# Negating and splitting the softmax maxima: ScalarE and GpSimd in place of VectorE

## The chip, the core and the metric

The kernel runs on one core of a Trainium2 chip, in one launch. The core has a matrix engine (TensorE, PE in the profile, with its weight loads as PEld), VectorE (DVE), ScalarE (ACT), GpSimd (POOL) and SyncE (SP), which here issues every transfer. Each engine runs its own queue in order and waits for the others by semaphores. The metric is the device time of one execution in microseconds (us), the median of several runs.

## The reference

One transformer block with adaptive layer norm on x of 2048 x 512 in float32, with 32 heads of 16 and a hidden width of 1792. Cut to what matters:

```python
h = layernorm(x) * (1 + ca) + sa                    # sa, ca, ga, ... from silu(c) @ w_mod
q, k, v = split(h @ wqkv)                           # 32 heads x 2048 x 16
p = softmax(einsum("bhqd,bhkd->bhqk", q, k) * 16 ** -0.5)
x = x + ga * (einsum("bhqk,bhkd->bhqd", p, v) @ wo)
h = layernorm(x) * (1 + cb) + sb
u = h @ w1 + b1
x = x + gb * ((u * tanh(softplus(u))) @ w2)
```

The softmax subtracts the largest score of each query before the exponential. That maximum is what the change is about.

## The kernel before

The scores are computed twice. A first pass (`max_tile`, product L471, reduction L473) computes tiles of 128 queries x 512 keys and takes each row's maximum on VectorE. A second pass (`score`, product L512) computes them transposed, 128 keys x 512 queries, and ScalarE takes the exponential straight out of PSUM (L520). The maximum has to be subtracted per query, which is a column there; so it goes in as two extra rows of the product's inner dimension: `qa` holds the minus maximum in rows 48 and 49 of each half, and `ka` holds ones. Products run in a format of reduced precision (float32r), so the number is split: row 48 takes the rounded minus maximum, row 49 what the rounding left.

Work is cut into 32 repeats, n = 0 to 31: a block of 512 queries (4 of them) times a group of four heads (8 of them). A repeat has 16 steps t, and step t has two half-steps 2t and 2t+1. In one step TensorE issues four score products of this repeat, four products of the maxima for a later repeat (the maxima run 20 steps ahead, `PRO`), a share of a unit of the projections or of the MLP (L132), and eight products with the values (L540, called by `pv`), which end the step. The score and maximum tiles take turns in a ring of six PSUM banks (`ring`); a product waits until the engine that reads the bank's last tile has done so. The program's order is the order in which the Python code records instructions; `at(h, f)` records f when the recording reaches half-step h. Nothing reorders it later.

Once a repeat, `neg_max` reduces the maxima to 128 x 32 (L482) and hangs `max_rows` on the end of step 16n-4, behind its L540 products and so just ahead of the next step's products. `max_rows` takes two ring banks, transposes the maxima on TensorE (L490), and turns them into `mt`, 32 rows of 128 numbers: sixteen rows of rounded minus maxima (`lows` is 0) and sixteen of remainders (`lows` is -1). `put` stands at half-step 32n-5 and sends `mt` with four transfers of 4 KB (L501) to rows 48 and 49 of the two `qa` tiles of repeat n, in the order (head pair 0, half 0), (0, 1), (1, 0), (1, 1). The scores of the repeat begin at step 16n, with half 1 of pair 0 and then half 1 of pair 1, so the second score product reads what the fourth transfer brings.

GpSimd meanwhile works through the MLP's activation: for each unit a clamp (L740), a product (L754, L755), a quotient (L770 to L774) and a split (L95, L98), each stage hung on its own half-step, with ScalarE's exponentials and logarithms (L746, L758, L761) between them. It also adds results to the residual (L893, which reads `yd`; ScalarE writes `yd` at L892, and there is one such buffer).

Of the kernel before, what the change touches and what calls it, by code (L numbers as in the profile page):

```python
# [8 lines left out]
F32 = mybir.dt.float32  # L9
F32R = mybir.dt.float32r  # L10
AF = mybir.ActivationFunctionType
ALU = mybir.AluOpType
# [6 lines left out]
def adaln_block(ctx: ExitStack, tc: tile.TileContext, x, wqkv, wo, w1, b1, w2, c, w_mod, out):  # L19
    nc = tc.nc  # L20
# [56 lines left out]
    lows = cst.tile([P, 1], F32, name="lows")  # L77
# [69 lines left out]
    def ring(w=1):  # L147
        if w == 2 and ring_at[0] % 2:
            ring_at[0] += 1
        b = ring_at[0] % NRING  # L150
        ring_at[0] += w
        return ring_t[:, b, :] if w == 1 else ring_t[:, b:b + 2, :]
# [32 lines left out]
    def at(h, f):  # L185

        hooks.setdefault(h, []).append(f)
# [289 lines left out]
    def neg_max(n):  # L477

        mx = mxs.pop(n)
        mm = ap.tile([P, 4, 2, 4], F32, tag="mm", name="mm", bufs=2)  # L480
        twice = bass.AP(tensor=mx.tensor, offset=mx.offset, ap=[list(mx.ap)[0], [16, 4], [0, 2], [4, 4], [1, 4]])
        nc.vector.tensor_reduce(out=mm, in_=twice, op=ALU.max, axis=AX.X)  # L482
        ats.setdefault(16 * n + 16 - PRO, []).append(lambda: max_rows(n, mm))

    def max_rows(n, mm):
        t = ring(2)
        cols = mm.rearrange("p a v q -> p (a v q)")
        for g in range(2):
            r = slice(64 * g, 64 * g + 64)
            nc.tensor.transpose(t[:32, g, :64], cols[r], ident[r, r])  # L490
        pt = t[:32, :, :64]
        mh, mt = [ap.tile([32, P], F32R, tag=n_, name=n_, bufs=1) for n_ in ("mh", "mt")]
        halves = [m.rearrange("p (g q) -> p g q", g=2) for m in (mh, mt)]
        nc.vector.tensor_scalar_mul(halves[0], pt, -1.0)
        nc.vector.scalar_tensor_tensor(halves[1], halves[0].bitcast(F32), lows[:32], pt, op0=ALU.mult, op1=ALU.subtract)

        def put():
            for j in range(2):
                for s in range(2):
                    o = (2 * s + j) * 8  # L500
                    nc.sync.dma_start(  # L501
                        qa[(2 * n + j) % NR][64 * s + 48:64 * s + 50, :].rearrange("v (s q) -> v s q", s=4).bitcast(F32),
                        mt[o:o + 8, :].bitcast(F32))
        at(2 * (16 * n + 16 - PRO) + 3, put)
# [835 lines left out]
    t = T + 2  # L1340
# [32 lines left out]
```

## Time and profile before

| what | value |
|---|---|
| median of 3 runs | 1700.25 us (1697.17 to 1701.53) |
| the profiled execution | 1693.26 us, its span 1691.5 us |
| granted TensorE clock | 0.996 |
| busy: TensorE, VectorE, ScalarE, GpSimd | 98%, 85%, 78%, 53% |
| a usual step of the long middle part | 2.84 us |
| L494 and L495 on VectorE | 32 times 279 ns and 335 ns |

A row of the timeline gives the start and the length in us, the engine, the line, what is written and read, and in brackets the idle time of that engine ahead of it with what ended it. A row of groups gives, after the bar, the busy time in us, the mean length in ns, and the idle time ahead. Line numbers are those of the kernel before; L494 and L495 are also, in the changed kernel, the two operations that take their place.

### The profile page before, as it was taken

Reading aid. Unit: us, or ns where it says so; the run is one execution under the profiler, and the core shown is the slowest. Engines: PE = TensorE matmul, PEld = TensorE weight load, DVE = VectorE, ACT = ScalarE, POOL = GpSimd, SP = SyncE. Lnnn points to the kernel's source line nnn. Section 1 sums busy time; section 2 is a strip of 40 time slices with the busy share of each in tenths; the row PEclk is TensorE's granted clock in tenths of the full one; section 3 lists DMA queues with packets and bytes.
Section 4 is the critical chain, followed back from the end, with each engine's and each line's share of the span. In section 5 each row is a group of like instructions: output and inputs, shape, how many; then the busy total and the mean of one; then the engine's idle time right before and its main releaser. Section 6 shows DMA issues by size and latency. Waiting matters only on the chain.

```text
span 1691.5 us, 32962 instructions
## 1 busy us (share of the span) xinstructions
PE 1660.6 (98%) x12316; PEld 921.7 (54%) x12316; DVE 1429.9 (85%) x2362; ACT 1327.1 (78%) x2559; POOL 898.0 (53%) x906
## 2 busy tenths in 40 slices
PE   6999999999999999999999999999999999999998
PEld 5755665554435455555555555555555555554687
DVE  6898898887998888988888888889888888881577
ACT  6247777777778898888889898888888898889264
POOL 5155215565504388755525498654535597646432
PEclk9999999999999999999999999999999999999999
DMA  7767457777772342434353644334442535332362
GB/s 249 192 224 215 120 159 213 250 226 226 232 210 63 111 123 74 127 80 149 86 133 74 197 105 99 99 109 123 117 103 79 176 95 131 93 107 82 132 218 74
DMA packets 113992, 240.03 MB, mean 142 GB/s; under 512 B 24048, under 2 KB 49648, under 8 KB 107784
## 3 DMA queue, kind: packets, MB, share of 16 engines
q1 hardware_dynamic: 113832, 237.92, 49.6%
q8 instruction: 97, 1.59, 0.4%
q14 instruction: 63, 0.52, 0.1%
HBM read 179.95 MB, written 51.44 MB: 137 GB/s over the span
## 4 chain that ended last, share of the span: by engine, by line
PE 92%; DVE 3%; DMA 2%; ACT 2%; SPq 1%; issue 1%; POOL 0%; DVEq 0%; ACTq 0%; POOLq 0%
PE bk L540 30%; PE ring L471 23%; PE ring L512 22%; PE bk L132 9%; PE bk L126 3%; PE ring L126 3%; PE ring L1074 2%; DVE mx L473 1%; ACT pr L520 1%; DMA xt<-in_A_x 1%; SPq L318 0%; DMA qa<-mt 0%; PE bk L1006 0%; DMA vg<-vscr 0%; PE ring L842 0%
## 5 line engine op out<-in xcount | busy, mean ns | idle before, releaser
L473 DVE TENSOR_REDUCE mx<-ring 128x1 f32<-128x512 f32 x2048 | 1276.1, 684 | 161.5 <-PE bk L132 104.9
L520 ACT ACTIVATE pr<-ring 128x512 f32<-128x512 f32 x2048 | 1090.2, 605 | 232.0 <-PE bk L132 168.8
L471 PE MATMUL ring<-ka,qa 64*128 64x512 f32 x2048 | 778.7, 427 | 0.5
L512 PE MATMUL ring<-qa,ka 64*128 64x512 f32 x2048 | 723.0, 397 | 7.8 <-ACT pr L520 4.6
L471 PEld LDWEIGHTS ring<-ka,qa 64*128 64x128 f32 x2048 | 366.5, 184 | 407.9 <-DVE mx L473 356.2
L540 PE MATMUL bk<-pr,vg 128*32 128x512 f32 x4096 | 545.9, 605 | 0.0
L512 PEld LDWEIGHTS ring<-qa,ka 64*128 64x128 f32 x2048 | 374.1, 184 | 120.8 <-ACT pr L520 35.6
L132 PE MATMUL bk<-h,w 64*128 64x512 f32 x1008 | 280.7, 410 | 0.0
L132 PE MATMUL bk<-w,a_h 64*128 64x512 f32 x576 | 194.8, 417 | 0.6 <-ACT pr L520 0.4
L132 PEld LDWEIGHTS bk<-h,w 64*128 64x128 f32 x1008 | 171.5, 184 | 5.7 <-ACT pr L520 0.4
L540 PEld LDWEIGHTS bk<-pr,vg 128*32 128x32 f32 x4096 | 81.0, 108 | 125.1 <-issue 117.0
L740 POOL TENSOR_SCALAR ee<-hb 128x512 f32<-128x512 f32 x42 | 62.5, 1488 | 96.7 <-ACT hb L734 88.2
L132 PE MATMUL bk<-w,a_l 64*128 64x512 f32 x288 | 113.7, 395 | 0.0
L770 POOL TENSOR_TENSOR ee<-ee,rr 128x512 f32<-128x512 f32 x42 | 53.9, 1284 | 111.6 <-ACT rr L761 111.4
L132 PEld LDWEIGHTS bk<-w,a_h 64*128 64x128 f32 x576 | 95.3, 185 | 5.2 <-ACT pr L520 1.5
L132 PE MATMUL bk<-w,o_hl 64*128 64x512 f32 x288 | 79.7, 409 | 0.0
L98 POOL TENSOR_TENSOR a_l<-hb,a_h 128x512 fp32r<-128x512 f32 x53 | 71.7, 1354 | 4.4
L893 POOL TENSOR_TENSOR y<-yd,y 128x512 f32<-128x512 f32 x40 | 51.4, 1285 | 35.5 <-ACT yd L892 35.3
L754 POOL TENSOR_SCALAR rr<-ee 128x512 f32<-128x512 f32 x42 | 26.1, 622 | 60.0 <-ACT ee L746 59.9
L132 PE MATMUL bk<-h_h,wl 64*128 64x512 f32 x168 | 57.5, 423 | 0.0
L95 POOL TENSOR_SCALAR a_h<-hb 128x512 fp32r<-128x512 f32 x53 | 36.3, 684 | 39.9 <-DVE hb L768 38.3
L774 POOL TENSOR_TENSOR hb<-hb,rr 128x512 f32<-128x512 f32 x42 | 54.5, 1298 | 3.3
(205 smaller groups left out, 1840.9 us busy)
## 6 DMA issues: line engine op xcount, KB each, us to landing
ka<-kscr SPq DMA_DIRECT2D x124, 384.0 KB
w<-w2scr SPq DMA_DIRECT2D x56, 512.0 KB
w<-w1scr SPq DMA_DIRECT2D x46, 512.0 KB
vg<-vscr SPq DMA_DIRECT2D x32, 552.0 KB
qa<-qscr SPq DMA_DIRECT2D x124, 100.0 KB
kscr<-qh SPq DMA_DIRECT2D x16, 512.0 KB
qscr<-qh SPq DMA_DIRECT2D x32, 256.0 KB
hl<-in_B_w SPq DMA_DIRECT2D x28, 256.0 KB
```

The costliest lines, as they stand in the source:

```text
L98: (nc.gpsimd if eng == "p" else nc.vector).tensor_sub(lo, src, hi.bitcast(F32))
L126: nc.tensor.matmul(acc, l, r, start=start, stop=stop)
L132: i = nc.tensor.matmul(acc, l[64 * g:64 * g + 64], r[64 * g:64 * g + 64], start=start, stop=stop)
L471: nc.tensor.matmul(pm, qt[64 * s:64 * s + 64, qs * P:(qs + 1) * P], kt[64 * s:64 * s + 64, kb * TB:(kb + 1) * TB], start=True, stop=True)
L473: return nc.vector.tensor_reduce(out=mxs[n][:, s, 4 * j + qs, kb:kb + 1], in_=pm, op=ALU.max, axis=AX.X)
L512: nc.tensor.matmul(p_, kt[64 * s:64 * s + 64, kc * P:(kc + 1) * P], qt[64 * s:64 * s + 64, :], start=True, stop=True)
L520: e = nc.scalar.activation(pr, p_, AF.Exp, scale=SCALE)
L540: nc.tensor.matmul(accs[n][32 * h:32 * h + 32, :], vgs[n][:, o:o + 32], pts.pop((t, h)), start=(kc == 0), stop=(kc == 15))
L740: nc.gpsimd.tensor_scalar_min(buf("ee", 2), b["hb"], HCAP)
L770: nc.gpsimd.tensor_mul(ee, ee, rr)
L774: nc.gpsimd.tensor_mul(hb, hb, rr)
L893: nc.gpsimd.tensor_add(y[i], yd, y[i])
```

## The change

The transposed maxima are no longer taken out of PSUM by VectorE. ScalarE copies them with a factor of -1, unrounded, into the memory of `mt`. GpSimd multiplies that by `lows` into `mh`, which rounds: minus the rounded number in the rows of remainders, and 0 in the others. It then adds the two into `mt`, in place.

```diff
-        pt = t[:32, :, :64]
         mh, mt = [ap.tile([32, P], F32R, tag=n_, name=n_, bufs=1) for n_ in ("mh", "mt")]
-        halves = [m.rearrange("p (g q) -> p g q", g=2) for m in (mh, mt)]
-        nc.vector.tensor_scalar_mul(halves[0], pt, -1.0)
-        nc.vector.scalar_tensor_tensor(halves[1], halves[0].bitcast(F32), lows[:32], pt, op0=ALU.mult, op1=ALU.subtract)
+        mc = mt.bitcast(F32)
+        nc.scalar.activation(mc.rearrange("p (g q) -> p g q", g=2), t[:32, :, :64], AF.Copy, scale=-1.0)
+        nc.gpsimd.tensor_scalar_mul(mh, mc, lows[:32])
+        nc.gpsimd.tensor_add(mt, mc, mh.bitcast(F32))
```

The order of everything else stays. VectorE's queue loses two instructions a repeat. Around repeat 14 it reads, before (`mx` are the row maxima, `mm` their reduction, `rc` a reciprocal of the softmax sums):

```order
L473 TENSOR_REDUCE mx<-ring 128x1 x20
L482 TENSOR_REDUCE mm<-mx 128x32
L473 TENSOR_REDUCE mx<-ring 128x1 x4
L494 TENSOR_SCALAR mh<-ring 32x128
L495 SCALAR_TENSOR_TENSOR mt<-mh,lows,ring 32x128
L473 TENSOR_REDUCE mx<-ring 128x1 x40
L575 RECIPROCAL rc<-sm 128x16
```

and with the change:

```order
L575 RECIPROCAL rc<-sm 128x16
L473 TENSOR_REDUCE mx<-ring 128x1 x20
L482 TENSOR_REDUCE mm<-mx 128x32
L473 TENSOR_REDUCE mx<-ring 128x1 x44
L575 RECIPROCAL rc<-sm 128x16
```

The reductions of the step after the transposes now follow those before it directly.

GpSimd's queue takes the pair in at the place where `max_rows` is recorded. At repeat 11 that is behind a quotient (`ee`, `rr`, `hb` are the activation's buffers, `a_h` and `a_l` its split result). Before:

```order
L772 TENSOR_TENSOR rr<-rr,ee 128x512
L773 TENSOR_TENSOR hb<-hb,ee 128x512
L774 TENSOR_TENSOR hb<-hb,rr 128x512
L740 TENSOR_SCALAR ee<-hb 128x512
L95 TENSOR_SCALAR a_h<-hb 128x512
L98 TENSOR_TENSOR a_l<-hb,a_h 128x512
```

and with the change:

```order
L772 TENSOR_TENSOR rr<-rr,ee 128x512
L773 TENSOR_TENSOR hb<-hb,ee 128x512
L774 TENSOR_TENSOR hb<-hb,rr 128x512
L494 TENSOR_SCALAR mh<-mt,lows 32x128
L495 TENSOR_TENSOR mt<-mt,mh 32x128
L740 TENSOR_SCALAR ee<-hb 128x512
L95 TENSOR_SCALAR a_h<-hb 128x512
```

What `put` sends now stands behind L774, and the clamp L740 of the next unit behind the pair.

At repeat 16 it is ahead of a quotient. Before (`y` is the residual's row):

```order
L754 TENSOR_SCALAR rr<-ee 128x512
L755 TENSOR_TENSOR ee<-ee,rr 128x512
L893 TENSOR_TENSOR y_5266<-yd,y_5266 128x512
L770 TENSOR_TENSOR ee<-ee,rr 128x512
L771 TENSOR_SCALAR rr<-rr 128x512
L772 TENSOR_TENSOR rr<-rr,ee 128x512
```

and with the change:

```order
L754 TENSOR_SCALAR rr<-ee 128x512
L755 TENSOR_TENSOR ee<-ee,rr 128x512
L893 TENSOR_TENSOR y_5274<-yd,y_5274 128x512
L494 TENSOR_SCALAR mh<-mt,lows 32x128
L495 TENSOR_TENSOR mt<-mt,mh 32x128
L770 TENSOR_TENSOR ee<-ee,rr 128x512
L771 TENSOR_SCALAR rr<-rr 128x512
```

The quotient, and all that follows on GpSimd, now stands behind the pair, and the pair behind ScalarE's copy. On ScalarE the copy (L493) stands behind the last exponential of step 16n-4 and ahead of the first of the next step. On TensorE no instruction moves; the product that takes the first of the two banks again waits for ScalarE instead of VectorE.

## The prediction

> **What bounds the kernel now.** I read the page's first part and its chain, then the lengths of single steps in the timeline, then the waits around the maxima.
>
> ```profile
> PE 1660.6 (98%) x12316; PEld 921.7 (54%) x12316; DVE 1429.9 (85%) x2362; ACT 1327.1 (78%) x2559; POOL 898.0 (53%) x906
> PE 92%; DVE 3%; DMA 2%; ACT 2%; SPq 1%; issue 1%; POOL 0%; DVEq 0%; ACTq 0%; POOLq 0%
> ```
>
> TensorE is busy for 98% of the span and is 92% of the chain that ended last. VectorE, which the change relieves, is 3% of that chain. So VectorE time is not worth its own length; it is worth what TensorE waits for it. The place to read is the step that follows `max_rows`. A step ends with eight products of line 540, so the starts of two such groups are one step apart. Here is TensorE around repeat n=14, and then the same rows of n=30, seventeen repeats from the one to the other:
>
> ```profile
> 746.15 1.06 PE L540 MATMUL bk<-pr,vg 128*32 128x512 f32 x8
> 747.15 0.23 PE L490 MATMUL ring<-ident,mm 64*32 64x64 f32 x2
> 749.18 1.06 PE L540 MATMUL bk<-pr,vg 128*32 128x512 f32 x8
> 752.02 0.64 PE L540 MATMUL bk<-pr,vg 128*32 128x512 f32 x4
> ...
> 1482.78 1.06 PE L540 MATMUL bk<-pr,vg 128*32 128x512 f32 x8
> 1485.82 1.07 PE L540 MATMUL bk<-pr,vg 128*32 128x512 f32 x8
> ```
>
> The step with the transposes (L490) takes 749.18-746.15 = 3.03 us, and 1485.82-1482.78 = 3.04 at the last; the next one takes 752.02-749.18 = 2.84. The excess is 0.19 us. What makes it:
>
> ```profile
> 747.14 0.09 PEld L490 LDWEIGHTS ring<-ident,mm 64*32 64x32 f32 x2 [0.84 <-DVE mx L473]
> 747.21 0.18 PEld L471 LDWEIGHTS ring<-ka,qa 64*128 64x128 f32 x1
> 748.75 0.18 PEld L512 LDWEIGHTS ring<-qa,ka 64*128 64x128 f32 x1 [0.29 <-DVE mx L473]
> ...
> 747.45 0.28 DVE L494 TENSOR_SCALAR mh<-ring 32x128 fp32r<-32x128 f32 x1
> 747.76 0.34 DVE L495 SCALAR_TENSOR_TENSOR mt<-mh,lows,ring 32x128 fp32r<-32x128 f32 x1
> 748.02 2.46 DVE L473 TENSOR_REDUCE mx<-ring 128x1 f32<-128x512 f32 x4
> ```
>
> The transposes push the next weights from 747.14 to 747.21: 0.07 us, which stays. The other 0.12 us is the wait at 748.75: the first reduction (L473) starts only when L495 is over, at 748.02, and gives its ring bank back late. Its product starts at 747.21 and needs 0.5 us, so without the two VectorE operations it could start near 747.72, 0.3 us earlier, which is as long as the wait of 0.29.
>
> **What the change takes away.** The two removed groups and the waits view of the stretch from 95 to 1530 us:
>
> ```profile
> L495 DVE SCALAR_TENSOR_TENSOR mt<-mh,lows,ring 32x128 fp32r<-32x128 f32 x32 | 10.7, 335 | 1.8 <-DVE mh L494 0.8
> L494 DVE TENSOR_SCALAR mh<-ring 32x128 fp32r<-32x128 f32 x32 | 8.9, 279 | 5.7 <-PE ring L490 2.7
> ...
> PEld ring L512 <- DVE mx L473: 10.3, 32, 0.8
> PEld ring L512 <- DVE mt L495: 4.4, 15, 0.5
> ```
>
> VectorE is rid of 10.7+8.9 = 19.6 us. The weight loader's waits that can go are 10.3+4.4 = 14.7 us at most, but while the loader waits an earlier product still runs, so the step's length decides: 0.12 us x 31 repeats = 3.7 us. The lower bound is nothing, the upper 14.7.
>
> The first repeat (n=0) is another case, since there, before the scores have begun, the chain of waits runs through VectorE itself:
>
> ```profile
> 97.33 0.20 DVE mh L494
> 97.55 0.34 DVE mt L495
> 97.89 12.57 DVE mx L473 x21
> ```
>
> Both operations are on the chain, 0.56 us from 97.33 to 97.89, and 21 reductions follow without a gap: 0.6 us more. Gain together: 4.3 us.
>
> **What it adds.** The trace has no copy of this size on ScalarE and no GpSimd operation of 128 elements with two tensors. The nearest rows:
>
> ```profile
> L272 ACT COPY vq<-bk 128x256 f32<-128x256 f32 x28 | 10.5, 374 | 22.1 <-PE bk L126 22.1
> L892 ACT COPY yd<-bk 128x512 f32<-128x512 f32 x49 | 28.8, 588 | 0.1
> L850 POOL TENSOR_SCALAR hf<-hf,modc 128x128 f32<-128x128 f32 x48 | 21.0, 452 | 3.9 <-ACT hf L847 3.5 <-PE bk L132 0.2 <-PE ring L471 0.2
> L625 POOL TENSOR_TENSOR wm<-wm 128x256 f32<-128x256 f32 x8 | 5.9, 736 | 0.6
> L98 POOL TENSOR_TENSOR hl<-hl 128x512 fp32r<-128x512 f32 x32 | 41.1, 1284 | 2.7
> L98 DVE TENSOR_TENSOR a_l<-hb,a_h 128x512 fp32r<-128x512 f32 x3 | 2.1, 693 | 0.3
> ```
>
> ScalarE: 374 ns for 256 elements and 588 for 512 make a straight line that gives 267 ns for 128 (bounds 160, the line's start, and 374). It lies in a gap:
>
> ```profile
> 746.09 1.56 ACT L520 ACTIVATE pr<-ring 128x512 f32<-128x512 f32 x3
> 747.98 1.09 ACT L520 ACTIVATE pr<-ring 128x512 f32<-128x512 f32 x2 [0.33 <-PE bk L132]
> ```
>
> ScalarE is idle for 0.33 us from 747.65 to 747.98, and the transposes end at 747.38, so the copy is taken at nothing. Behind it in ScalarE's queue are the next step's exponentials, and TensorE waits for the first of them; if the copy were to start only at 747.65 and last 374 ns, they would be 0.04 us late, 1.3 us in all.
>
> GpSimd: the scalar operation at 0.45 (L850 has 128 elements too), the sum at 0.46 (the line through 736 and 1284), and twice 0.08 for the step from one to the next: 1.07 us a pair. 32 x 1.07 = 34 us on an engine that is 53% busy hide unless somebody waits. Bounds: twice 0.19 (what the lines leave at no elements), and 1.35 for each as for the sums of 512.
>
> A rule of the Trainium skill speaks against this part: its page GPSIMD Engine Reference, section Engine selection, sends elementwise work to VectorE, since GpSimd is about 2x slower with two inputs. The rows agree (1284 against 693 ns). By that rule alone the pair would take twice VectorE's 0.61 us, 1.23 plus the steps between, and the sum below would come out 1.6 us worse.
>
> Now who waits for the pair. It stands in GpSimd's queue behind all that was recorded ahead of `max_rows`, and the transfers of L501 wait for it, in SP's queue. In most repeats GpSimd is at the pair before ScalarE has written; then mt is ready at 747.92+1.07 = 748.99 instead of 748.10, and the transfers start 0.9 us later, which the rows below show to be covered: 4.9 us lie between the last landing and the product that reads it. Not so at n=11, and at 19 and 27, which have the same place in the next blocks:
>
> ```profile
> 613.83 1.30 POOL L774 TENSOR_TENSOR hb<-hb,rr 128x512 f32<-128x512 f32 x1
> 610.81 2.82 SPq L501 DMA_DIRECT2D qa<-mt  x4
> 613.68 0.39 SPq L666 DMA_DIRECT2D w<-w1scr  x1
> 614.25:614.45 0.20, 0.20 (x6) 0.20 (x2) 0.20 (x1) 0.20 (x1) 0.20 (x1) 1.00 0.08 21
> 619.33 0.39 PE L512 MATMUL ring<-qa,ka 64*128 64x512 f32 x1
> ```
>
> The pair now follows L774, which ends at 615.13. So mt is ready at 616.20 instead of 610.8, the four issues of 2.82 us end at 619.02, and the last lands 0.82 us behind them, as now (the issues end at 613.63, its bytes move until 614.45): 619.84. The second score product of the new repeat (L512 at 619.33) reads that one. With the 0.12 us won before, it stands for 619.84-619.21 = 0.63, say 0.7 us with the signal. Three times: 2.1 us. Behind it in SP's queue the weights of L666 go 5.4 us later; they fill the half that has just been freed, a unit ahead of use. The far bound for such a transfer is this wait on the chain at n=6, among heavy traffic:
>
> ```profile
> 382.29 6.10 DMA qa<-mt
> ```
>
> At n=5 to 7 GpSimd is busy at that place as well, but the traffic lands these transfers late anyway: I allow 0.3 us for the three (bounds 0, and for each the pair behind one sum of 512, 1.07+1.28 = 2.4).
>
> At n=16, and 24 likewise, the pair stands ahead of L770:
>
> ```profile
> 838.70 0.23 PE L490 MATMUL ring<-ident,mm 64*32 64x64 f32 x2
> 837.89 1.28 POOL L770 TENSOR_TENSOR ee<-ee,rr 128x512 f32<-128x512 f32 x1 [6.83 <-ACT rr L761]
> 843.81 1.28 POOL L893 TENSOR_TENSOR y<-yd,y 128x512 f32<-128x512 f32 x1
> 846.31 0.59 ACT L892 COPY yd<-bk 128x512 f32<-128x512 f32 x1
> 848.16 2.06 ACT L520 ACTIVATE pr<-ring 128x512 f32<-128x512 f32 x4 [0.27 <-PE bk L132]
> ```
>
> GpSimd, which now starts L770 at 837.89, holds it back until the transposes of 838.70 are copied (about 839.45) and the pair is done: 840.5, 2.6 us later. Up to L893 it has no gap, so L893 ends at 847.7 instead of 845.09. L892 on ScalarE overwrites yd, which L893 reads: from 846.31 to 847.7, 1.4 us late, with two exponentials behind it. ScalarE has 0.27 us of idle before the next step; 1.1 us reaches TensorE, twice: 2.2 us. At the other repeats GpSimd's lateness is hidden by the half-steps of 1.42 us that the hooks leave between the stages of a unit; if that cover were gone, a repeat would cost 1.1 us like this one.
>
> **The sum.** Cost 2.1+0.3+2.2 = 4.6, gain 4.3: +0.3 us. The profiled execution took 1693.26 us (span 1691.5), 7 us under the median of the runs, 1700.25. So 1693.6 on its scale and 1700.5 on theirs. A measurement of this kernel can tell about 0.3%, 5.1 us; I forecast no change.
>
> **Rivals.** (1) GpSimd becomes what the others wait for: slower. The mechanism is the pair in the queue; the point is its length, since five repeats (11, 19, 27, 16, 24) pass on each us of it. Twice my price, 2.14 us, adds 5.4, and the upper bounds, 2x1.35+0.16 = 2.86 us, add 9.0; the middle is 7.2 us: 1707.7. For it: the price has no row, and the order of the queue is bad at those places. Against: rows of 128 and 256 elements lie close. The skill's GpSimd rule, above, points this way. (2) The loader's waits are worth their full length: 14.7+0.6-4.6 = 10.7 us faster, 1689.6. For it: 32 waits on the very reduction that is delayed. Against: steps of 3.03 beside 2.84, of which 0.07 stays. (3) The change does not do what it says: ScalarE comes late with the copy, so the banks come back no sooner; only the costs stay, 4.6 us, 1704.9. For it: ScalarE is 78% busy. Against: the gap of 0.33 us.
>
> **How the numbers follow.** Forecast 0.53, with its own range 1695 to 1705 (gain and cost each wrong by up to 5 us); rival (1) 0.27; (2) 0.14; (3) 0.06, half of it over the 0.3%. Slower is 0.27+0.03 = 0.30, faster 0.14 and a little of the forecast's low end, 0.16, the same 0.54. The range reaches up past rival (1) to 1709 and down to 1692, which leaves out most of rival (2) and the far end of (1).
>
> **What would show it.** Right: the step with the transposes falls from 3.03 to 2.91; the wait of L512 for mx of 32 times is gone; the pair's two rows near 0.45 each; at n=11, 19, 27 the wait on qa<-mt, 0.7 us; at n=16 and 24 L892 waiting for L893 on GpSimd. Wrong: pairs of 2 us, waits on GpSimd at more than five repeats, or exponentials that start later after the transposes than now, 0.83 us.

## The result and the profile after

The changed kernel takes 1702.24 us (median of 20 runs, 1695.77 to 1707.86), the kernel before 1698.69 us (20 runs beside them, 1691.92 to 1702.67). The ratio is 1.0026, with a 95% interval from 1.0015 to 1.0036: 4.4 us slower (2.5 to 6.1); the two medians themselves lie 3.6 us apart. The forecast was 1700.5 us and no change; the time lies 1.7 us above it, inside the range and inside the 0.3% that were called the same, but the sign of the small rest is clear. The profiled execution took 1698.16 us, its span 1696.4 us.

The page after the change, busy time and the chain by engine:

```profile
PE 1660.4 (98%) x12316; PEld 927.8 (55%) x12316; DVE 1416.3 (83%) x2298; ACT 1333.2 (79%) x2591; POOL 930.4 (55%) x970
PE 91%; DVE 2%; DMA 2%; ACT 2%; POOL 1%; issue 1%; SPq 0%; DVEq 0%; POOLq 0%; ACTq 0%
```

VectorE has 13.6 us less to do (not the 19.6 us of its two operations: its reductions L473 alone went from 1276.1 to 1280.0), GpSimd 32.4 us more, and GpSimd, at 0% before, now has 1% of the chain. The groups of the three new operations (busy us, mean ns of one, idle time ahead):

```profile
L494 POOL TENSOR_SCALAR mh<-mt,lows 32x128 fp32r<-32x128 f32 x32 | 19.1, 598 | 78.6 <-ACT mt L493 78.4
L495 POOL TENSOR_TENSOR mt<-mt,mh 32x128 fp32r<-32x128 f32 x32 | 14.4, 451 | 2.7
L493 ACT ACTIVATE mt<-ring 32x128 f32<-32x128 f32 x32 | 8.3, 258 | 5.5 <-PE ring L490 3.2 <-issue 1.3 <-ACT pr L520 0.6
```

The gain first: the timeline around repeat 14, the same place as before the change, and the waits of the weight loader from 95 to 1535 us:

```profile
749.43 1.06 PE L540 MATMUL bk<-pr,vg 128*32 128x512 f32 x8
750.42 0.23 PE L490 MATMUL ring<-ident,mm 64*32 64x64 f32 x2
750.80 0.25 ACT L493 ACTIVATE mt<-ring 32x128 f32<-32x128 f32 x1
751.03 2.58 DVE L473 TENSOR_REDUCE mx<-ring 128x1 f32<-128x512 f32 x4 [0.42 <-PE ring L471]
751.26 1.09 ACT L520 ACTIVATE pr<-ring 128x512 f32<-128x512 f32 x2 [0.21 <-PE bk L132]
752.35 1.07 PE L540 MATMUL bk<-pr,vg 128*32 128x512 f32 x8
...
PEld ring L512 <- DVE mx L473: 4.2, 7, 1.2
```

The step takes 752.35-749.43 = 2.92 us, where it took 3.03. The first reduction starts 751.03-750.42 = 0.61 us after the transposes, where it was 748.02-747.15 = 0.87, and waits for its product instead of for VectorE. The 32 waits on that reduction are down to 7. The exponentials start 0.84 us after the transposes, 0.83 before: ScalarE's copy is hidden.

Then the places where time is lost. Repeat 11:

```profile
616.16 1.29 POOL L774 TENSOR_TENSOR hb<-hb,rr 128x512 f32<-128x512 f32 x1
617.44 0.59 POOL L494 TENSOR_SCALAR mh<-mt,lows 32x128 fp32r<-32x128 f32 x1
618.12 0.45 POOL L495 TENSOR_TENSOR mt<-mt,mh 32x128 fp32r<-32x128 f32 x1
618.60 2.81 SPq L501 DMA_DIRECT2D qa<-mt  x4
618.66 1.49 POOL L740 TENSOR_SCALAR ee<-hb 128x512 f32<-128x512 f32 x1
619.76 1.06 PE L540 MATMUL bk<-pr,vg 128*32 128x512 f32 x8
620.17 0.63 ACT L746 ACTIVATE ee<-ee 128x512 f32<-128x512 f32 x1 [0.89 <-POOL ee L740]
622.57 0.18 PEld L512 LDWEIGHTS ring<-qa,ka 64*128 64x128 f32 x1 [0.56 <-DMA qa<-mt]
623.72 1.06 PE L540 MATMUL bk<-pr,vg 128*32 128x512 f32 x8
```

The step is 623.72-619.76 = 3.96 us instead of 2.84. Two things are late in it: the transfers, which wait for the pair behind L774, and ScalarE's L746, which waits for the clamp L740 behind the pair. Repeat 16, where the pair stands ahead of the quotient:

```profile
842.29 0.60 POOL L494 TENSOR_SCALAR mh<-mt,lows 32x128 fp32r<-32x128 f32 x1 [8.38 <-ACT mt L493]
843.40 1.27 POOL L770 TENSOR_TENSOR ee<-ee,rr 128x512 f32<-128x512 f32 x1
849.15 1.07 PE L540 MATMUL bk<-pr,vg 128*32 128x512 f32 x8
849.32 1.29 POOL L893 TENSOR_TENSOR y<-yd,y 128x512 f32<-128x512 f32 x1
850.64 0.59 ACT L892 COPY yd<-bk 128x512 f32<-128x512 f32 x1 [1.48 <-PE ring L471]
851.28 0.49 PE L132 MATMUL bk<-w,a_h 64*128 64x512 f32 x1 [0.64 <-ACT yd L892]
853.19 1.06 PE L540 MATMUL bk<-pr,vg 128*32 128x512 f32 x8
```

ScalarE's L892 starts at 850.64, when L893 on GpSimd has ended (849.32+1.29 = 850.61), after 1.48 us of idle; the step is 853.19-849.15 = 4.04 us. (The row puts that wait down to an earlier product; the one that ended last is L893. In a second profile of this kernel the same wait, 1.46 us, is put down to L893.) The last repeat, n=31, shows one more, which the prediction did not name:

```profile
1546.56 1.06 PE L540 MATMUL bk<-pr,vg 128*32 128x512 f32 x8
1550.22 1.06 PE L540 MATMUL bk<-pr,vg 128*32 128x512 f32 x8
...
1548.15 0.63 ACT L746 ACTIVATE ee<-ee 128x512 f32<-128x512 f32 x1 [0.77 <-POOL ee L740]
```

3.66 us, where the same step was 2.77.

All the steps can be measured like this, by the starts of the groups of L540. The table gives them for every kernel of this study. "Late part" is the time from the 136th group to the last, in n=8 to 31. In two profiles of the changed kernel and in three of the one before its steps agree within 0.1 us.

| kernel | step with transposes, mean of 30 | first step, n=11, 19, 27 | first step, n=16, 24 | late part, us | ratio to before |
|---|---|---|---|---|---|
| before (3 profiles) | 3.09 to 3.10 | 2.84 | 2.84 | 1064.1 to 1064.5 | |
| changed (2 profiles) | 2.92 | 3.92 to 4.00 | 4.01 to 4.04 | 1067.7, 1068.2 | 1.0026 |
| VectorE splits | 4.10 | 2.84 | 2.84 | 1091.1 | 1.0199 |
| transfers reordered | 2.94 | 3.45 | 4.00 | 1067.8 | 1.0025 |
| pair left out | 2.92 | 2.84 | 2.84 | 1061.2 | 0.9976 |
| pair made longer | 2.92 | 5.67 to 6.22 | 5.38, 5.89 | 1090.2 | 1.0168 |
| ten repeats old | 2.98 | 2.84 | 2.84 | 1062.3, 1062.7 | 0.9985, 0.9988 |
| six repeats old | 2.95 | 2.84 | 2.84 | 1062.1 | 0.9999 |

In the late part the change costs 3.6 us: three times 1.13, twice 1.2 and 0.9 make 6.7, and 22 steps with transposes give 3.1 back.

### The profile page after: what moved, and what is told of

It reads as the page before. It is cut to its first block, busy times and chain, and to the rows that moved or that the text cites. A ratio compares the mean times of both kernels' runs of the same rounds, so it can differ in the third digit from the quotient of the medians.

```text
span 1696.4 us, 33072 instructions
## 1 busy us (share of the span) xinstructions
PE 1660.4 (98%) x12316; PEld 927.8 (55%) x12316; DVE 1416.3 (83%) x2298; ACT 1333.2 (79%) x2591; POOL 930.4 (55%) x970
## 4 chain that ended last, share of the span: by engine, by line
PE 91%; DVE 2%; DMA 2%; ACT 2%; POOL 1%; issue 1%; SPq 0%; DVEq 0%; POOLq 0%; ACTq 0%
PE bk L540 29%; PE ring L471 23%; PE ring L512 21%; PE bk L132 9%; PE bk L126 3%; PE ring L126 3%; PE ring L1074 2%; ACT pr L520 1%; DMA qa<-mt 1%; DMA wma<-in_w_mod 1%; DVE mx L473 1%; DVE hf L374 0%; PE bk L1006 0%; PE ring L842 0%; PE ring L1006 0%
## 5 line engine op out<-in xcount | busy, mean ns | idle before, releaser
L473 DVE TENSOR_REDUCE mx<-ring 128x1 f32<-128x512 f32 x2048 | 1280.0, 685 | 183.5 <-PE bk L132 107.9
L540 PE MATMUL bk<-pr,vg 128*32 128x512 f32 x4096 | 545.9, 605 | 0.0
L540 PEld LDWEIGHTS bk<-pr,vg 128*32 128x32 f32 x4096 | 81.0, 108 | 125.3 <-issue 117.3
L740 POOL TENSOR_SCALAR ee<-hb 128x512 f32<-128x512 f32 x42 | 62.5, 1488 | 91.3 <-ACT hb L734 82.6
L770 POOL TENSOR_TENSOR ee<-ee,rr 128x512 f32<-128x512 f32 x42 | 53.9, 1284 | 71.5 <-ACT rr L761 71.2
L98 POOL TENSOR_TENSOR a_l<-hb,a_h 128x512 fp32r<-128x512 f32 x53 | 71.7, 1353 | 4.4
L893 POOL TENSOR_TENSOR y<-yd,y 128x512 f32<-128x512 f32 x40 | 51.5, 1287 | 28.0 <-ACT yd L892 28.0
L494 POOL TENSOR_SCALAR mh<-mt,lows 32x128 fp32r<-32x128 f32 x32 | 19.1, 598 | 78.6 <-ACT mt L493 78.4
L774 POOL TENSOR_TENSOR hb<-hb,rr 128x512 f32<-128x512 f32 x42 | 54.5, 1298 | 3.3
```

What stands on the lines that cost most here:

```text
L98: (nc.gpsimd if eng == "p" else nc.vector).tensor_sub(lo, src, hi.bitcast(F32))
L473: return nc.vector.tensor_reduce(out=mxs[n][:, s, 4 * j + qs, kb:kb + 1], in_=pm, op=ALU.max, axis=AX.X)
L540: nc.tensor.matmul(accs[n][32 * h:32 * h + 32, :], vgs[n][:, o:o + 32], pts.pop((t, h)), start=(kc == 0), stop=(kc == 15))
L740: nc.gpsimd.tensor_scalar_min(buf("ee", 2), b["hb"], HCAP)
L770: nc.gpsimd.tensor_mul(ee, ee, rr)
L774: nc.gpsimd.tensor_mul(hb, hb, rr)
```

## The experiments

**VectorE splits (dve_split).** Is the gain the reduction that no longer stands behind VectorE's operations, or the ring banks that come free sooner? ScalarE copies as in the change; the pair goes back to VectorE, at the same place.

```diff
-        nc.gpsimd.tensor_scalar_mul(mh, mc, lows[:32])
-        nc.gpsimd.tensor_add(mt, mc, mh.bitcast(F32))
+        nc.vector.tensor_scalar_mul(mh, mc, lows[:32])
+        nc.vector.tensor_add(mt, mc, mh.bitcast(F32))
```

> ScalarE copies as in the change, but VectorE does the multiplication and the sum, at the same place in the program. Theory: the gain is the first reduction that no longer waits behind VectorE's two operations. Then the gain is lost here and more, since they now also wait for the copy: the reduction starts some 0.4 us later than before the change and the step with the transposes takes 3.3 to 3.5 us, 30 times, so 8 to 14 us slower than before. Rival: the gain is the ring banks, which ScalarE frees sooner; then the step stays near 2.9 and the time is 4 to 5 us under before, as no one waits for GpSimd.

Measured: 1729.52 us, ratio 1.0199 (1.0181 to 1.0216), and the six long steps are back at their length before the change (2.83 to 2.85, and 2.76 at n=31), while the step with the transposes is far longer. So the gain hangs on VectorE's place in front of the reduction; that ScalarE frees the ring banks does not by itself keep the step short. Where GpSimd was idle the step came out at 3.27, near the expected 3.3 to 3.5, as at 525 us:

```profile
524.08 1.06 PE L540 MATMUL bk<-pr,vg 128*32 128x512 f32 x8
525.68 0.28 DVE L494 TENSOR_SCALAR mh<-mt,lows 32x128 fp32r<-32x128 f32 x1 [0.41 <-ACT mt L493]
525.99 0.28 DVE L495 TENSOR_TENSOR mt<-mt,mh 32x128 fp32r<-32x128 f32 x1
527.35 1.06 PE L540 MATMUL bk<-pr,vg 128*32 128x512 f32 x8
```

Elsewhere it was far longer, up to 4.9 us, and that nobody had expected:

```profile
713.73 0.62 POOL L754 TENSOR_SCALAR rr<-ee 128x512 f32<-128x512 f32 x1
713.77 0.66 DVE L494 TENSOR_SCALAR mh<-mt,lows 32x128 fp32r<-32x128 f32 x1 [0.48 <-ACT mt L493]
714.44 1.27 POOL L755 TENSOR_TENSOR ee<-ee,rr 128x512 f32<-128x512 f32 x1
714.47 1.38 DVE L495 TENSOR_TENSOR mt<-mt,mh 32x128 fp32r<-32x128 f32 x1
716.50 0.50 PE L512 MATMUL ring<-qa,ka 64*128 64x512 f32 x1 [1.64 <-DVE mx L473]
```

Each of the two VectorE operations, where it starts while GpSimd is at work, ends just after GpSimd's operation: for L495, 714.47+1.38 = 715.85 and 714.44+1.27 = 715.71. More on this at the end.

**Transfers reordered (order).** At n=11 the profile shows the second score product waiting for the fourth transfer. The four transfers were issued in the order in which the products read them.

```diff
-            for j in range(2):
-                for s in range(2):
+            for s in (1, 0):
+                for j in range(2):
                     o = (2 * s + j) * 8
```

> The changed kernel with the four transfers in the order in which the products read them: half 1 of both head pairs first, half 0 after. Theory: at n=11, 19, 27 and 5 to 7 the second score product waits for the fourth transfer; as second it lands 1.4 us earlier. Then n=11, 19, 27 are back at 2.84 us (from 3.96 to 4.00), n=5 to 7 lose 3 to 5 us together, n=16 and 24 stay at 4.0: 6 to 8 us under the changed kernel, 2 to 4 under the one before. Rival: the wait is for the pair itself, whatever the order; then nothing moves by more than 0.5 us.

Measured: 1701.0 us, ratio 1.0025 (1.0012 to 1.0038), the same as the change without it. The theory fell. The waits on the transfers are gone from the late part (1.7 us in 3 waits of the loader in the changed kernel, none now), and the repeat still loses its time, in another coin: 3.45 us in the first step, 0.62 more than before the change, and 0.36 and 0.19 more in two later ones, 1.2 us against 1.1. What was under the transfers:

```profile
621.67 0.45 POOL L495 TENSOR_TENSOR mt<-mt,mh 32x128 fp32r<-32x128 f32 x1
622.21 1.49 POOL L740 TENSOR_SCALAR ee<-hb 128x512 f32<-128x512 f32 x1
623.72 0.63 ACT L746 ACTIVATE ee<-ee 128x512 f32<-128x512 f32 x1 [0.87 <-POOL ee L740]
624.89 0.18 PEld L512 LDWEIGHTS ring<-qa,ka 64*128 64x128 f32 x1 [0.38 <-ACT pr L520]
```

GpSimd's clamp is late by the pair, ScalarE's exponential of the MLP waits for it, and the softmax exponentials stand behind that in ScalarE's queue.

**Pair left out (no_split_half).**

```diff
-        nc.scalar.activation(mc.rearrange("p (g q) -> p g q", g=2), t[:32, :, :64], AF.Copy, scale=-1.0)
-        nc.gpsimd.tensor_scalar_mul(mh, mc, lows[:32])
-        nc.gpsimd.tensor_add(mt, mc, mh.bitcast(F32))
+        nc.scalar.activation(mt.rearrange("p (g q) -> p g q", g=2), t[:32, :, :64], AF.Copy, scale=-0.5)
```

> The changed kernel with the GpSimd pair left out: ScalarE's copy, with a factor of -0.5, writes mt, and the transfers wait for that alone (both rows hold half the negated maximum; the remainder is not formed). If all costs come from the pair on GpSimd and the gain from VectorE's relief, the step with the transposes stays at 2.90, the first steps at n=11, 16, 19, 24, 27 are back at 2.84 and n=31 loses its 0.9: about 5 us under the kernel before (ratio 0.997). If ScalarE's copy itself costs something, n=16, 24 and 31 keep a part.

Measured: 1692.92 us, ratio 0.9976 (0.9966 to 0.9987), 4.1 us under the kernel before. All six long steps are back at their old length, and the step with the transposes stays at 2.92. So the six losses are the pair's, ScalarE's copy costs nothing, and 4 us is what the change could bring if the split were free.

**Pair made longer (double).**

```diff
         nc.gpsimd.tensor_scalar_mul(mh, mc, lows[:32])
+        nc.gpsimd.tensor_scalar_mul(mh, mc, lows[:32])
+        nc.gpsimd.tensor_scalar_mul(mh, mc, lows[:32])
```

> The changed kernel with the multiplication on GpSimd done three times, 1.36 us more for each pair (twice 0.60 and the step of 0.08). Theory (at six repeats the others wait for GpSimd, which passes on each us): first steps of 5.3 to 5.4 at n=11, 16, 19, 24, 27, from 3.96 to 4.04, some 2.2 at n=31; the tight places behind (n=14, 15, 22, 23, 30) begin to show some tenths. 8 to 12 us over the changed kernel. Rival (the cost is the wait for ScalarE's copy in GpSimd's queue, or the transfers, and not the length): n=16 and 24 grow by less than 0.5 us each, and the total by less than 5.

Measured: 1724.93 us, ratio 1.0168 (1.0155 to 1.0181), 28.5 us over the kernel before and 24 over the changed one: twice to three times what was expected. The theory holds in kind. Repeat 11:

```profile
624.84 1.06 PE L542 MATMUL bk<-pr,vg 128*32 128x512 f32 x8
626.62 0.63 ACT L748 ACTIVATE ee<-ee 128x512 f32<-128x512 f32 x1 [2.25 <-POOL ee L742]
630.69 1.93 PE L542 MATMUL bk<-pr,vg 128*32 128x512 f32 x8
```

ScalarE now waits 2.25 us for the clamp (line numbers are two higher here), 1.36 more than 0.89: the length is passed on whole. The step is 5.85 us now, 1.89 more than the 3.96, and the one behind it takes 1.0 more than before the change; the transfers go out 1.4 us later too (625.04-622.00 = 3.04 us behind a group of products, 618.60-616.92 = 1.68 in the changed kernel), but what makes the loss larger than 1.36 was not followed. And places that had slack lose it. ScalarE's waits for GpSimd from 500 to 1600 us, in the changed kernel and here:

```profile
ACT ee L746 <- POOL ee L740: 3.5, 4, 0.9
ACT rr L758 <- POOL ee L755: 2.1, 1, 2.1
ACT yd L892 <- POOL y L893: 1.5, 1, 1.5
```

```profile
ACT ee L748 <- POOL ee L742: 10.9, 6, 2.3
ACT rr L760 <- POOL ee L757: 5.7, 6, 1.0
ACT yd L894 <- POOL y L895: 5.6, 2, 2.8
```

Eight more places show a loss: six of 0.8 us, in the last steps of n=12, 13, 20, 21, 28 and 29, three steps behind the pair that belongs to the next repeat, and two of 1.1 to 1.2 in the second steps of n=15 and 23. The changed kernel stands close to an edge: with 1.1 us a pair six pairs are paid for, with 2.5 us fourteen.

**Ten repeats old (mixed, and once more as mixed_again).** VectorE's two operations stay in the repeats where GpSimd is late (11, 16, 19, 24, 27, 31), in the heavy traffic (5, 6, 7) and at the start (0).

```diff
+        if n in (0, 5, 6, 7, 11, 16, 19, 24, 27, 31):
+            ...
+            nc.vector.tensor_scalar_mul(halves[0], pt, -1.0)
+            nc.vector.scalar_tensor_tensor(halves[1], ...)
+        else:
+            ...
+            nc.gpsimd.tensor_add(mt, mc, mh.bitcast(F32))
```

> The changed kernel, but with VectorE's two old operations in the ten repeats n = 0, 5, 6, 7, 11, 16, 19, 24, 27, 31, and the new form in the other 22. Theory (the cost hangs on the place in GpSimd's queue, the gain on each repeat): steps of 2.90 after the 22, of 3.03 to 3.25 after the ten, no first step longer than before the change; 20 to 22 times 0.13 to 0.17, some 3 us under the kernel before (ratio 0.998). Rival (the pair costs by its length, wherever it stands): other repeats now show the waits, and nothing is gained.

> The mixed kernel (old form at n = 0, 5, 6, 7, 11, 16, 19, 24, 27, 31) a second time, since its first interval ended just under 1. By the steps that two profiles of one kernel have in common, it wins 2.0 us from n=8 on and about 1 us before: ratio 0.998, with an interval under 1 if the first result holds; 1.000 if that was chance.

Measured: 1693.04 us, ratio 0.9985 (0.9973 to 0.9997), and in the second comparison 1693.21 us, 0.9988 (0.9977 to 0.9999). This version beats both kernels, the one before by 2.0 to 2.5 us, though both intervals end just under 1. Repeat 11, at its transposes and at its first step (the group of L540 is L546 here):

```profile
609.62 1.06 PE L546 MATMUL bk<-pr,vg 128*32 128x512 f32 x8
612.73 1.06 PE L546 MATMUL bk<-pr,vg 128*32 128x512 f32 x8
...
618.41 1.06 PE L546 MATMUL bk<-pr,vg 128*32 128x512 f32 x8
621.25 1.07 PE L546 MATMUL bk<-pr,vg 128*32 128x512 f32 x8
```

The step with the transposes takes 3.11 us in the old form, 0.08 more than in the kernel before, and at n=19 even 3.43; why was not tried. The first step is at 2.84.

**Six repeats old (six_old).** The same with the list (11, 16, 19, 24, 27, 31).

> The changed kernel with VectorE's two old operations at n = 11, 16, 19, 24, 27, 31 alone. Theory: these six are the whole lasting cost (1.13 to 1.2 us each at five, 0.9 at n=31), and the other 26 keep their gain of 0.12 to 0.35; n=0 and n=5 to 7 then carry only the noise of their traffic. 2 to 5 us under the kernel before (ratio 0.997 to 0.999). Rival: n=5 to 7 cost 3 us by the pair; then no better than the kernel before.

Measured: 1696.32 us, ratio 0.9999 (0.9989 to 1.0008). The late part is that of the ten (1062.1 us), so these six are the whole cost there. The total is the same as that of the kernel before: the 2 to 5 us that were expected did not come, and the result is the one that the rival named. By the ratios the ten are some 2 us better than the six, though the intervals overlap. What difference there is must lie in n=0 to 8, which the next three runs are about.

**The kernels once more (after_again, before_again, before_third).**

> The changed kernel once more, for a second profile. Steps that differ between two profiles of one kernel are noise of the transfers. Expected the same within 0.1 us: 2.90 at the transposes, 3.96 to 4.04 at n=11, 16, 19, 24, 27, 0.9 at n=31. Expected to differ by some us: n=5 to 8, where the transfers are in heavy traffic.

> The kernel before once more, for a second profile. The steps of n=5 to 8 are in question: in the first profile they exceed 2.84 us by 5.1 us together, in the changed kernel's two by 8 to 10. If that is noise of the traffic, this profile shows 6 to 10 as well; if the change costs 3 us or more there, it shows 4 to 6.

> The kernel before a third time, for the same question and with the same expectations: 6 to 10 us over the usual steps at n=5 to 8 if the difference there is noise, 4 to 6 if the change costs 3 us there. Elsewhere all steps within 0.1 us of the first profile.

Measured: the changed kernel's second profile repeats the six long steps within 0.07 us. At n=5 to 8 everything moves. The other steps of these repeats, those with transposes left out, exceed 2.84 us by 3.2, 6.7 and 5.9 us in the three profiles of the kernel before, by 6.8 and 8.4 in those of the changed one, and by 9.3 where the pair is left out. The first profile of the kernel before was a lucky one. From the second, the waits of the weight loader for the transfers from 320 to 500 us:

```profile
PEld ring L512 <- DMA qa<-mt: 6.3, 3, 3.6
```

The loader's three waits come to 6.3 us here; in the changed kernel's first profile it was 6.0 us in three. So in the kernel before the traffic alone can make them. In the changed kernel the pair is late there as well. At n=7, with the transposes at 425.65:

```profile
432.99 0.45 POOL L495 TENSOR_TENSOR mt<-mt,mh 32x128 fp32r<-32x128 f32 x1
433.46 2.80 SPq L501 DMA_DIRECT2D qa<-mt  x4
```

`mt` is ready 7.8 us after the transposes and the transfers follow at once; in the kernel before it is ready after 0.9 us, and SP's queue holds the transfers until 1.7, 6.4 and 6.6 us in the three profiles. Over all twelve profiles of this study the excess is 3.2 to 6.7 us in the six in which VectorE splits the maxima at n=5 to 7 (before, dve_split, mixed) and 6.8 to 11.1 us in the other six. The two groups nearly touch, but they speak for a cost of some us at these repeats. It cannot be the pair alone, since leaving it out shows 9.3; what it is stays open.

## Why the prediction was right, and where it was not

The sum said +0.3 us and the measurement says +4.4 (2.5 to 6.1). Both are "the same" by the 0.3% bound, but not by the same terms, and that the time came so close is in part luck. The forecast of 1700.5 us stood on a median of three runs; on the 1698.69 us of the twenty it would have been 1699.0, 3.2 us under the measurement. The gain and the cost were both set too low, and the two errors made up for each other in part. Of the signs, "right" showed at the step with the transposes, at the loader's 32 waits (7 are left) and at n=16 and 24; one of the signs for "wrong" showed too, waits on GpSimd at more than five repeats.

- **The step with the transposes**, 3.03 to 2.91: it went to 2.92, by the mechanism named; dve_split and no_split_half show it. The term was too small: the average over 30 steps is 3.09 to 2.92, 0.17 and not 0.12, so 5.1 us and not 3.7. Repeat 14 was taken for all, and steps of 3.20 to 3.27 also came down to 2.85 to 2.91.
- **The start**, 0.6 us to be won at n=0: it did not show. GpSimd comes to the pair at 100.55 behind three sums of L98 and a copy. From the transposes of n=0 to the first group of L540 it is 17.0 and 16.5 us in the changed kernel's profiles and 16.2, 17.2 and 16.3 in those of before.
- **The copy on ScalarE**, priced at 267 ns and hidden: 258 ns, and hidden.
- **The pair**, priced at 0.45+0.46 and two steps of 0.08, 1.07 us: 0.60+0.45, and from its start to that of the next operation 1.22 us at n=11 and 1.11 at n=16. The upper bound of 1.35 us, given "as for the sums of 512", is in no row: those sums take 1.28 to 1.30 in the mean. GpSimd stands ready for the copy in 14 of the 32 repeats, not in most. The doubling by the rule of the Trainium skill was applied to both operations, though the rule as cited is for two inputs; here the sum takes 451 ns beside 278 to 280 in dve_split, and the multiplication, with one tensor as input, 598 beside 273 to 275 where nothing holds it up. The wait on GpSimd at n=16 and 24 was priced at 1.1 us each and was 1.2.
- **n=11, 19, 27**, 0.7 us each by the transfers: 1.1 us each, and here a step of the argument failed: who waits for the pair. Only the consumer that the trace showed to be near was followed, the transfers; the next operation in GpSimd's own queue, the clamp L740, and ScalarE behind it were put under "hidden by the half-steps". Once the transfers were out of the way (order) that chain took the same time, so it is enough alone. That the transfers alone would be enough no run shows. The second score product, which waits last for them, starts 622.58-619.76 = 2.82 us behind the group of L540, where it was 619.33-617.53 = 1.80, so 1.0 us late, not 0.6 to 0.7.
- **n=31** was left out altogether, for the same reason: 0.9 us. There the pair makes L770 wait for ScalarE's copy (it starts at 1536.81, its input had been ready since 1534.5), and L740 and L746 follow late.
- **n=5 to 7**, 0.3 us: open, and probably too low. The shown steps make 3.6 us in the late part, less 2.1 from eight steps with transposes ahead of it, so 1.5 us. The other 1.0 to 4.6 us of the measured interval must then lie in the transfers of n=5 to 8 or at the start, where profiles of one kernel differ by up to 3.5 us. The excess at n=5 to 8 is 7.6 us in the mean of the changed kernel's two profiles and 5.3 in that of the three before, 2.3 us more. The version with the old form at n=0, 5, 6 and 7 too has the better times, while no_split_half, without any pair, shows a larger excess there than the changed kernel. No cause is shown, and this part of the cost may be larger than the 1.5 us that is explained.

Of the rivals, the first (GpSimd becomes what others wait for) names the mechanism that decides the late part: six repeats pass on the pair's length, and more of them as it grows. Its price was wrong, since the pair was nearly as short as the forecast had it. The second (the loader's waits at full length, 10.7 us) fell: with the pair left out 4.1 us is all there is. So did the third: the copy is not late.

## What to carry to other kernels

An engine that is busy half the time can still be the one that others wait for: what a small operation costs there is decided by what stands behind it in that queue, and each consumer of the next few operations has to be followed, not just the reader of the result. When removing a wait leaves the time unchanged, look for a second one of the same size under it, with the same origin. And a change that wins at most places and loses at a few can be made at the places where it wins: here that turned +4.4 us into some -2.

## What the hardware showed that was not expected

In dve_split the two VectorE operations, which there read the maxima from SBUF, are held up by a GpSimd operation that is under way when they start. The 16 sums of L495 that met no GpSimd operation took 278 to 280 ns, and the 16 that met one took 0.56 to 1.39 us, ending 0.13 to 0.14 us after it; L494, 273 to 275 ns alone, took up to 1.16 us and, where it was held up, ended 0.07 to 0.08 us after it. The Trainium skill, page SBUF — State Buffer, section SBUF: two separate sides, says that the two engines share a pair of ports as an exclusive lock, held for a whole instruction by whichever comes first, and that on VectorE's side this goes for operations with two inputs from SBUF or in a two-port mode. For L495, which has two inputs, the trace agrees; which of the two L494 is, it does not show. Not every VectorE operation on SBUF is held up: the reduction L482, with one input, took 285 to 289 ns in all 32 repeats of the kernel before, GpSimd busy beside it in 23 of them. The operations of the kernel before, which take one input from PSUM, never showed it: 269 to 281 ns and 333 to 339 ns over all 32 repeats, with GpSimd busy beside many of them. Reading the maxima straight from PSUM was worth more than it looked, though no run changed that alone.

The multiplication on GpSimd takes 0.60 us for 32x128, while one of 128x128 (L850) takes 0.45. What makes the smaller one slower was not tried.
